# Attention values by quarters of the array: 128 keys from two blocks, two banks

## The chip, the cores and the metric

One core of a Trainium2 chip runs the whole program. The metric is the device time of one execution in microseconds (us), the median over the runs. The profile is that of one further execution; its span runs from the first to the last instruction.

## The reference, cut to what matters

Attention over a sliding window of 128 keys with a linear distance penalty, followed by a feed-forward block with squared ReLU, all in fp32:

```python
B, H, S, D = 8, 8, 576, 64
mask = (rel >= 0) & (rel < 128)              # rel = query position - key position
scores = where(mask, q @ k.T / sqrt(D) + bias, -1e9)
attn = softmax(scores)
x = (attn @ v)            # -> [B*S, 512] = [4608, 512]
h = relu(x @ w_in)        # w_in  [512, 2048]
out = (h * h) @ w_out     # w_out [2048, 512]
```

## The kernel before, in words

The 4608 tokens of all batches are cut into 9 chunks of 512 (`c`), the 8 heads into 4 pairs (`p`), the 2048 hidden columns into 16 tiles (`f`). A chunk and a pair make a **couple** `q = 4c + p`, which holds two **segments** of 256 tokens (`sg` 0 and 1). There are 36 couples. In a segment a tile of 128 tokens (`i` = 0, 1) for each head (`j` = 0, 1) attends to 128 keys for every token: those of its own 128-key block up to its own place, and the later part of the block before.

The feed-forward part is `gemm1(c, f)`, 12 matmuls of 512 columns into the PSUM tile `g` (pool `g1`, one bank), and `gemm2(c, f)`, 12 matmuls in four groups `m` of three, into four PSUM tiles `acc`. After `gemm1`, ScalarE takes the ReLU of `g` (L178), VectorE squares it (L184), ScalarE casts the high part `hh` (L186), VectorE subtracts for the low part `hl` (L188). Both GEMMs run in fp32r with such splits. The other PSUM pools are `sc` (two banks, tile `s` or `S`), `at` (one bank) and `ac` (four).

The first four couples and the next four run in `start`, from a plan with costs and due times. From then on the loop over `t` in `tile_attn_moe` sets TensorE's order by hand: an even `t` is a `gemm1`, an odd `t` the `gemm2` of two tiles earlier. Eight steps of `t` make one **round**, in which one couple passes through. In the round's step `part == 0` come, ahead of `gemm2`: `both`, which computes the values of the couple whose softmax is done (28 couples go this way, from couple 8 on); the loads of the couple after next; and `Couple.front`, the scores and the softmax of the next couple (27 couples). At `part` 3 and 5 `middle` transposes a segment's probabilities on TensorE (L302), ScalarE copies them to `own` (L309), and two GpSimd selects make `prev` (L312) and `own` (L318), zero outside the window. The other engines' instructions are ordered by the framework.

`mix` (L327 to L338) computes the values: for each tile `i` and head `j` one matmul with the 128 keys of the block before (`prev`) and one with the 128 keys of the own block (`own`), each of 128 token columns, 64 output rows, all 128 rows of the array. The two heads use the two column halves. An fp32 product stands in the trace as two matmul records, called passes here. `both` then casts the high part of the result on ScalarE (L359) and subtracts for the low part on VectorE (L360); tile `xu` is what `gemm1` reads.

`Couple.scores` computes products of 64 rows by 64 output rows with 64, 128 or 192 columns, in a **quarter** of the array each: `h` picks the output half, `j` (the head) the row half. The list of each quarter is laid end to end by columns, `at` being the place where a product begins, and all are issued in the order of `at`. The scores of segment 1 that stand in `base` share the bank `G` (from pool `g1`) between both heads: `shared`. So that two row halves never write it together, the second head's first product in it waits for a GpSimd nop (L412) that waits for the first head's last (`done`). Blocks that lie in another batch's window are left out (`late`), so that couples come in seven kinds, three or four couples of each.

ScalarE then copies the base scores to SBUF (L441, L448), VectorE folds in the rest (L460, L464), finds the row maxima (L276), ScalarE exponentiates (L283), VectorE inverts the sums (L290, L291), GpSimd normalises (L294).

Of the kernel before, what the change touches and what calls it, by code (L numbers as in the profile page):

```python
# [9 lines left out]
F32 = mybir.dt.float32  # L10
F32R = mybir.dt.float32r
# [3 lines left out]
ALU = mybir.AluOpType  # L15
# [5 lines left out]
NP = H // 2  # L21
# [12 lines left out]
LATER = [("z", 7)]  # L34
RING = lambda k: 55 + 10.5 * (k - 8)
CONV = lambda f: 36 + 6 * f
FIRST = 35
SYNC = mybir.DependencyInfo(mybir.DependencyClass.Sync, mybir.DependencyReason.DATA)
CST = 256 + 128 * H
ENGINES = {e: getattr(mybir.EngineType, e) for e in ("PE", "DVE", "Activation", "Pool", "SP")}  # L40
# [6 lines left out]
class Kern:  # L47
# [67 lines left out]
    def load_qk(self, c, p, sg):  # L115
# [7 lines left out]
            to, of = to[:, a:e], of[:, a:e]  # L123
        self.nc.sync.dma_start(to, of)

    def load_v(self, c, p):
        self.v[c, p] = self.room(c, p, "v", [128, 5, 128], 4608)
        a = 0 if c else 128
        self.nc.sync.dma_start(self.v[c, p].rearrange("p n d -> p (n d)")[:, a:640], self.vd[c, p][:, a:640])
# [31 lines left out]
    def gemm1(self, c, f):  # L161
        nc = self.nc
        xs = [self.x[c, p] for p in range(NP)]
        g = self.g1.tile([128, 512], F32, name="g")
        wh, wl = self.w[f][:, 0, :, 1], self.w[f][:, 0, :, 0]
        i = 0
        for cc in range(NCC):
            for w, part in ((wh, 0), (wh, 1), (wl, 0)):
                nc.tensor.matmul(  # L169
                    g, w[:, cc * 128 : cc * 128 + 128], xs[cc][:, part], start=i == 0, stop=i == 11  # L170
                )
                i += 1
        yield
        r = self.hp.tile([128, 512], F32, name="r", bufs=1)
        hh = self.hp.tile([128, 512], F32R, name="hh")
        hl = self.hp.tile([128, 512], F32R, name="hl")
        self.h[c, f] = hh, hl
        nc.scalar.activation(r, g, AF.Relu)  # L178
        if c == 0:
            yield  # L180
            nc.scalar.activation(r, r, AF.Square)
        else:
            yield
            nc.vector.tensor_tensor(r, r, r, op=ALU.mult)  # L184
        yield
        nc.scalar.copy(hh, r)  # L186
        yield
        nc.vector.tensor_tensor(hl, r, hh.bitcast(F32), op=ALU.subtract)  # L188

    def gemm2(self, c, f):  # L190
        nc = self.nc
        hh, hl = self.h.pop((c, f))
        if f == 0:
            self.acc = self.start_banks if c == 0 else [self.ac.tile([128, 512], F32, name="acc") for _ in range(4)]
        wh, wl = self.w[f][:, 1, :, 1], self.w[f][:, 1, :, 0]
        for m in range(4):
            ms = slice(m * 128, m * 128 + 128)
            for i, (w, h) in enumerate(((wh, hh), (wh, hl), (wl, hh))):
                nc.tensor.matmul(  # L199
                    self.acc[m], w[:, ms], h, start=(f == 0 and i == 0), stop=(f == NF - 1 and i == 2)  # L200
                )
            if f == NF - 1:
                o = self.op.tile([128, 512], F32, name="o")
                out = self.outd[m * 128 : m * 128 + 128, 512 * c : 512 * c + 512]
                if c == NCH - 1 and m == 3:
                    nc.scalar.copy(o[:, 0:256], self.acc[m][:, 0:256])
                    nc.vector.tensor_copy(o[:, 256:512], self.acc[m][:, 256:512])
                    nc.sync.dma_start(out[:, 0:256], o[:, 0:256])
                    nc.scalar.dma_start(out[:, 256:512], o[:, 256:512])
                    continue  # L210
                (nc.scalar.copy if m % 2 else nc.vector.tensor_copy)(o, self.acc[m])
                nc.sync.dma_start(out, o)


class Segment:
# [86 lines left out]
            self.nc.tensor.transpose(self.z[:, m], self.t[:, m], self.K.ident)  # L302

    def place(self):
        pp = self.K.pp.tile([128, 1024], F32, name="pp")
        self.own, self.prev = (pp[:, a : a + 512].rearrange("p (m c) -> p m c", c=128) for a in (0, 512))

    def out(self):
# [40 lines left out]

    def both(self, other):
        K = self.K
        X = K.at.tile([128, 512], F32, name="at")
        for s in (self, other):
            s.X = X[:, 256 * s.sg : 256 * s.sg + 256]
            s.mix(s.sg == 0)
        u = K.x[self.c, self.p] = K.xu.tile([128, 2, 512], F32R, name="xu")
        self.nc.scalar.copy(u[:, 0], X)  # L359
        self.nc.vector.tensor_tensor(u[:, 1], X, u[:, 0].bitcast(F32), op=ALU.subtract)  # L360

    def soft(self):
        for m in range(4):
# [2 lines left out]
        self.sums()  # L366
        self.norm()

    def middle(self):
        self.turn()  # L370
        self.out()
        self.before()
        self.same()


class Couple:
# [11 lines left out]
    def scores(self):  # L388
        K, nc = self.K, self.nc
        self.S = K.sc.tile([128, 2, 512], F32, name="s")  # L390
        self.G = K.g1.tile([128, 512], F32, name="g")
        todo = []
        for h in range(2):
            base, extra = (h, h + 1), (2 - 2 * h,)
            for j in range(2):
                first = [(0, i, p) for i in range(2) for p in ([(0, 1, 2)] if h == 0 else [base, extra])]
                shared, rest = ([(1, i, p) for i in range(2)] for p in (base, extra))
                at = 0
                for s, i, part in shared + first + rest if j == 0 else first + rest + shared:
                    blocks = [x for x in part if x >= self.both[s].late.get(2 * i + h, 0)]  # L400
                    if blocks:
                        to, n = self.spot(s, j, i, part == extra), len(blocks)
                        a = 64 * (blocks[0] - part[0])
                        todo.append((at, h, j, s, i, blocks[0], n, to[64 * h : 64 * h + 64, a : a + 64 * n], s == 1 and part == base))
                        at += 64 * n
        done = None
        qk = K.qk[self.both[0].c, self.both[0].p]
        for at, h, j, s, i, a, n, to, shared in sorted(todo, key=lambda y: y[:3]):
            u, r = 4 * s + 2 * i + h, slice(64 * j, 64 * j + 64)
            q0, k0 = 64 * u + 640 * s, 256 + 64 * (u + a)  # L410
            if shared and j == 1 and done:
                turn = nc.gpsimd.nop()  # L412
                K.tc.add_manual_dep(turn.ins, done.ins.name, SYNC, reason="one head at a time in the shared bank")
            mm = nc.tensor.matmul(  # L414
                to, qk[r, q0 : q0 + 64], qk[r, k0 : k0 + 64 * n], start=True, stop=True, skip_group_check=True,
            )
            if shared and j == 0:
                done = mm
            elif shared and done:
                K.tc.add_manual_dep(mm.ins, turn.ins.name, SYNC, reason="one head at a time in the shared bank")  # L420
                done = None
# [173 lines left out]
def start(K):  # L595
# [31 lines left out]
    for k in range(18):  # L627
# [19 lines left out]
        else:  # L647
# [6 lines left out]
                P.add(n("e", m), "Activation", 0.4, (n("t", m),) + ((n("e", m - 1),) if m else ()), d + 0.5, do(G.exp, m))  # L654
            P.add(n("r"), "DVE", 0.4, (n("e", 3),), d + 1, G.sums)
            P.add(n("n"), "Pool", 1.05, (n("r"),), d + 1, G.norm)
            if k > 16:
                continue
            P.add(n("z"), "PE", 0.55, (n("n"),) + chain("z"), d + 1, G.turn, ("at", "pp"), "t")
            P.add(n("o"), "Activation", 0.6, (n("z"),), d + 1, G.out, None, "at")  # L660
            P.add(n("p"), "Pool", 0.72, (n("o"),), d + 1.5, G.before)
            P.add(n("m"), "Pool", 0.66, (n("p"),), d + 1.5, G.same)
            if k > 15:
                continue
            P.add(n("x"), "PE", 1.1, (n("m"), ("v", c, p)) + chain("x"), d + 2, G.values, "at", "pp")
            P.add(n("h"), "Activation", 0.4, (n("x"),), d + 2, G.high)
            P.add(n("l"), "DVE", 0.36, (n("h"),), d + 2, G.low, None, "at")
# [27 lines left out]
def tile_attn_moe(ctx: ExitStack, tc: tile.TileContext, *aps):  # L695
    K = Kern(ctx, tc, *aps)
    K.const()
    with tc.manual_schedule(engines={ENGINES["PE"]}):
# [3 lines left out]
        for n in range(NF, NF * NCH + 2):  # L702
            for t in (2 * n, 2 * n + 1):
                q, part = divmod(t - FIRST, 8)
                q += 9
                with tc.high_priority(offset=50):
                    if part == 0:
                        if q - 1 in pairs:
                            first, second = pairs.pop(q - 1)
                            first.both(second)  # L710
                        if q + 1 < 4 * NCH:
                            K.load(*divmod(q + 1, 4))
                        if q < 4 * NCH:
                            C = Couple(K, q)
                            C.front()
                            pairs[q] = C.both
                    if part in (3, 5) and q in pairs:
                        pairs[q][part // 4].middle()
                if t % 2 == 0 and n < NF * NCH:
                    for _ in K.gemm1(*divmod(n, NF)):  # L720
                        pass
                if t % 2:
                    K.gemm2(*divmod(n - 2, NF))


def _consts():
# [16 lines left out]
def _arrays(q, k, v, moe_w_in, moe_w_out):  # L743
# [6 lines left out]
    ], axis=2) for c in range(NCH)])  # L750
    vt = np.zeros((NP, 1 + B * S // 128, 128, 128), np.float32)
    vt[:, 1:] = v.reshape(B, NP, 2, S, D).transpose(1, 0, 3, 2, 4).reshape(NP, B * S // 128, 128, 128)
    vd = np.stack([vt[:, 4 * c : 4 * c + 5].transpose(0, 2, 1, 3).reshape(NP, 128, 640) for c in range(NCH)])
    w1d = a(moe_w_in.reshape(NCC, 128, NF, 128).transpose(2, 1, 0, 3).reshape(NF, 128, NCC * 128))
    return [a(qkd), a(vd), w1d.view(np.int64), a(moe_w_out).view(np.int64), _consts()]

# [17 lines left out]
```

## Time and profile before

| what | us |
|---|---|
| median of 3 runs | 997.23 (997.16 to 998.27) |
| the profiled execution | 996.04 |
| its span | 994.2 |
| TensorE busy | 984.2 (99%) |
| VectorE, ScalarE, GpSimd busy | 438.4, 453.7, 191.8 |

The busy share of TensorE is modelled, since the ends of pipelined matmuls are; the starts of its records show its pace. The profiled execution is 1.84 us longer than its span.

### The profile page before, as it was taken

The numbers are of one execution on the slowest core, as the hardware profiler recorded it, in microseconds if no ns is written. First come the engines' busy times: TensorE is split into PE (matmuls) and PEld (weight loads), VectorE is DVE, ScalarE is ACT, GpSimd is POOL, SyncE is SP. The second block draws the span as 40 slices with busy tenths as digits, with TensorE's granted clock in tenths as the row PEclk, the third lists the DMA queues.
The fourth block names the chain that finished last, engine by engine and source line by source line (L and its number), as shares of the span: only waits on it lengthen the run. The fifth ranks groups of instructions, "written<-read, shape, count | busy, mean of one in ns | idle before, by whom it ended". The sixth has DMA issues, their size and how long they took to land.

```text
span 994.2 us, 16896 instructions
## 1 busy us (share of the span) xinstructions
PE 984.2 (99%) x6545; PEld 814.1 (82%) x6548; DVE 438.4 (44%) x1269; ACT 453.7 (46%) x1180; POOL 191.8 (19%) x252
## 2 busy tenths in 40 slices
PE   9899999999999999999999999999999999999998
PEld 5678788888888888888888888888888888888886
DVE  6889824444443434344444344333434444422222
ACT  7899744444433444344444343334444444422221
POOL 4132321221112222222212211122222221100000
PEclk9999999999999999999999999999999999999999
DMA  9971202111211002111211121110111110001001
GB/s 350 404 276 53 63 14 80 38 39 38 80 38 39 26 20 73 39 38 38 81 38 38 38 80 38 38 39 19 65 35 39 38 57 1 1 1 43 1 1 42
DMA packets 26943, 61.50 MB, mean 62 GB/s; under 512 B 2928, under 2 KB 4336, under 8 KB 26864
## 3 DMA queue, kind: packets, MB, share of 16 engines
q1 hardware_dynamic: 26432, 59.91, 17.4%
q8 instruction: 51, 0.84, 0.3%
q10 hardware_dynamic: 432, 0.52, 0.2%
q14 instruction: 28, 0.23, 0.1%
HBM read 50.99 MB, written 9.44 MB: 61 GB/s over the span
## 4 chain that ended last, share of the span: by engine, by line
PE 97%; DVE 1%; ACT 1%; issue 0%; POOL 0%; DVEq 0%; POOLq 0%; ACTq 0%
PE acc L199 41%; PE g L169 40%; PE at L335 6%; PE at L302 3%; PE s L414 2%; PE g L414 2%; PE g L105 1%; PE s L239 1%; PE acc L335 1%; PE at L530 0%; PE s L498 0%; PE acc L498 0%; PE acc L533 0%; DVE tw L508 0%; ACT w L155 0%
## 5 line engine op out<-in xcount | busy, mean ns | idle before, releaser
L169 PE MATMUL g<-xu,w 128*128 128x512 f32 x1728 | 433.9, 400 | 2.6 <-ACT r L178 2.6
L199 PE MATMUL acc<-hh,w 128*128 128x512 f32 x1152 | 388.7, 398 | 0.0
L169 PEld LDWEIGHTS g<-xu,w 128*128 128x128 f32 x1728 | 333.3, 196 | 65.3 <-ACT r L178 3.3
L199 PEld LDWEIGHTS acc<-hh,w 128*128 128x128 f32 x1152 | 224.8, 195 | 46.1 <-issue 1.5
L184 DVE TENSOR_TENSOR r<-r 128x512 f32<-128x512 f32 x128 | 88.6, 692 | 342.3 <-ACT r L178 340.4
L199 PE MATMUL acc<-hl,w 128*128 128x512 f32 x576 | 227.6, 395 | 0.0
L178 ACT ACTIVATE r<-g 128x512 f32<-128x512 f32 x144 | 85.5, 594 | 299.5 <-PE g L169 299.2
L188 DVE TENSOR_TENSOR hl<-r,hh 128x512 fp32r<-128x512 f32 x144 | 102.2, 710 | 108.9 <-ACT hh L186 104.7
L186 ACT CAST hh<-r 128x512 fp32r<-128x512 f32 x144 | 89.2, 619 | 95.0 <-DVE r L184 94.5
L199 PEld LDWEIGHTS acc<-hl,w 128*128 128x128 f32 x576 | 112.5, 195 | 20.4
L294 POOL TENSOR_TENSOR t<-t,nm 128x512 f32<-128x512 f32 x64 | 81.1, 1267 | 239.2 <-DVE nm L291 214.2
L283 ACT ACTIVATE t<-t,nm 128x128 f32<-128x128 f32 x256 | 99.5, 390 | 35.2 <-DVE nm L276 35.0
L312 POOL TENSOR_SCALAR_AFFINE_SELECT pp<-pp 128x512 f32<-128x512 f32 x64 | 43.4, 679 | 185.7 <-ACT pp L309 185.6
L335 PEld LDWEIGHTS at<-pp,v 128*64 128x64 f32 x1024 | 55.2, 137 | 12.7 <-issue 12.0
L335 PE MATMUL at<-pp,v 128*64 128x128 f32 x1024 | 63.8, 276 | 0.0
L309 ACT COPY pp<-at 128x512 f32<-128x512 f32 x72 | 42.1, 584 | 45.5 <-PE at L302 44.5
L276 DVE CUSTOM_DVE_ANT_0 t<-t,cst 128x128 f32<-128x128 f32 x256 | 59.2, 293 | 1.0
L450 POOL MEMSET t<- 64x128 f32 (+1 forms) x35 | 8.1, 232 | 236.3 <-PE g L414 235.9
L460 DVE COPY_PREDICATED t<-cst,s 64x256 f32<-64x256 int32 x85 | 37.8, 445 | 32.4 <-ACT t L448 19.1
L283 ACT ACTIVATION_READ_ACCUMULATOR t<-t,nm 128x1 f32 x256 | 48.0, 187 | 0.0
L318 POOL TENSOR_SCALAR_AFFINE_SELECT pp<-pp 128x512 f32<-128x512 f32 x64 | 42.3, 661 | 4.4
L414 PE MATMUL s<-qk 64*64 64x64 f32 (+2 forms) x988 | 40.2, 253 | 0.0
(71 smaller groups left out, 587.4 us busy)
## 6 DMA issues: line engine op xcount, KB each, us to landing
raw<-in_dram SPq DMA_DIRECT2D x32, 512.0 KB, 8.9
qk<-in_dram SPq DMA_DIRECT2D x32, 320.0 KB, 3.5
v<-in_dram SPq DMA_DIRECT2D x32, 320.0 KB, 3.0
qk<-in_dram SPq DMA_DIRECT2D x38, 256.0 KB, 3.8
out_dram<-o SPq DMA_DIRECT2D x35, 256.0 KB, 2.7
v<-in_dram SPq DMA_DIRECT2D x3, 256.0 KB, 5.0
wide<-in_dram SPq DMA_DIRECT2D x3, 256.0 KB, 5.2
qk__200<-in_dram SPq DMA_DIRECT2D x2, 256.0 KB, 5.6
```

The costliest lines, as they stand in the source:

```text
L169: nc.tensor.matmul(g, w[:, cc * 128 : cc * 128 + 128], xs[cc][:, part], start=i == 0, stop=i == 11)
L178: nc.scalar.activation(r, g, AF.Relu)
L184: nc.vector.tensor_tensor(r, r, r, op=ALU.mult)
L186: nc.scalar.copy(hh, r)
L188: nc.vector.tensor_tensor(hl, r, hh.bitcast(F32), op=ALU.subtract)
L199: nc.tensor.matmul(self.acc[m], w[:, ms], h, start=(f == 0 and i == 0), stop=(f == NF - 1 and i == 2))
L276: self.nc.vector.tensor_tensor_reduce(self.t[:, m], self.t[:, m], self.K.nrel(2 * self.p + m // 2), -0.125, BIG, ALU.add, ALU.min, self.nm ...
L283: self.nc.scalar.activation(self.t[:, m], self.t[:, m], AF.Exp, bias=nm[:, m : m + 1], scale=-1.0, accum_out=nm[:, 4 + m : 5 + m],)
L294: self.nc.gpsimd.tensor_tensor(self.t, self.t, self.nm[:, 8:12].unsqueeze(2).to_broadcast([128, 4, 128]), op=ALU.mult)
L312: self.nc.gpsimd.affine_select(self.prev, self.own, pattern=[[0, 4], [-1, 128]], compare_op=ALU.is_gt, fill=0.0, base=0, channel_multiplier=1,
L335: self.nc.tensor.matmul(self.X[r, o : o + 128], v[:, 2 * sg + k, r], src[:, j], start=start and n == 0, stop=n == 3 - self.skip, skip_grou ...
L414: mm = nc.tensor.matmul(to, qk[r, q0 : q0 + 64], qk[r, k0 : k0 + 64 * n], start=True, stop=True, skip_group_check=True,)
```

## The change

- The values are computed in two kinds of product. `wholes`: the own block, one product of 128 rows and 128 columns for each `i` and `j`, as before. `corners`: the block before is no longer multiplied in 128 rows. For each `i`, `j` and each half `h` of the rows one product of 64 rows, 64 output rows and 64 columns, so that one token half meets one key half. Corners of `h` = 0 go to the bank `X`, in which the wholes are added; those of `h` = 1 go to a second bank `Y`, taken from the pool `g1`.
- For every token half, the probabilities for 128 keys from two blocks now lie in `own` and in the new tile `rest`, which four smaller GpSimd selects in `halves` make out of `own`, in place of two in `middle`.
- The values `vd` of chunks 2 and up are stored so that rows 64 and up of each block hold those of the block one earlier.
- `both` evacuates by two more steps: VectorE copies `Y` to SBUF (`first`) and adds half of `X` to it, ScalarE copies the other half of `X`; then the cast and the subtraction as before, now out of SBUF. `hl` of the `gemm1` just ahead is ordered behind `first`.
- `both` and `front` move from ahead of `gemm2` to behind its first group of three matmuls, and a round begins two steps of `t` later (`FIRST`). `middle` of segment 16 moves from `start` into the loop.
- In `Couple.scores` the head that uses the shared bank first is now `j` = 1, and its shared products stand behind one other product in the list.

```diff
-FIRST = 35
+FIRST = 37
+ORDER = mybir.DependencyInfo(mybir.DependencyClass.NoSync, mybir.DependencyReason.SCHED_ONLY)
...
+    def parts(self, s):
+        return s.pp[:, 512:768].rearrange("p (m c) -> p m c", c=64)
...
+    def halves(self):
+        nc = self.nc
+        self.turn()
+        self.out()
+        self.rest = self.K.parts(self)
+        for to, of, sign in ((self.rest, self.own, 1), (self.own, self.own, -1)):
+            for h in range(2):
+                r, c = slice(64 * h, 64 * h + 64), slice(64 * h, 64 * h + 64)
+                d = sign * (1 - 2 * h)
+                nc.gpsimd.affine_select(
+                    to[r] if to is self.rest else to[r, :, c], of[r, :, c], pattern=[[0, 4], [-d, 64]],
+                    compare_op=ALU.is_gt if d > 0 else ALU.is_ge, fill=0.0, base=0, channel_multiplier=d,
+                )
+    def corners(self, X, Y):
+        K, sg = self.K, self.sg
+        v, rest = K.v[self.c, self.p], self.rest.rearrange("p (j i) c -> p j i c", j=2)
+        for i in range(2):
+            n = 2 * sg + i
+            for h, to, k in ((0, X[:, 256 * sg + 128 * i :], n), (1, Y[:, 128 * sg + 64 * i :], (n + 2) % 5)):
+                r = slice(64 * h, 64 * h + 64)
+                for j in range(2):
+                    d = slice(64 * j, 64 * j + 64)
+                    self.nc.tensor.matmul(
+                        to[d, 0:64], v[r, k, d], rest[r, j, i], start=h == 1 or n == 0, stop=True, skip_group_check=True,
+                    )
+    def wholes(self, X):
+        K, sg = self.K, self.sg
+        v, own = K.v[self.c, self.p], self.own.rearrange("p (j i) c -> p j i c", j=2)
+        for i in range(2):
+            n = 2 * sg + i
+            for j in range(2):
+                d = slice(64 * j, 64 * j + 64)
+                self.nc.tensor.matmul(
+                    X[d, 128 * n : 128 * n + 128], v[:, n + 1, d], own[:, j, i], start=False, stop=True,
+                    skip_group_check=True,
+                )
     def both(self, other):
...
+        Y = K.g1.tile([128, 512], F32, name="g")
+        u = K.x[self.c, self.p] = K.xu.tile([128, 2, 512], F32R, name="xu")
+        low = K.op.tile([128, 512], F32, name="o")
         for s in (self, other):
-            s.X = X[:, 256 * s.sg : 256 * s.sg + 256]
-            s.mix(s.sg == 0)
-        u = K.x[self.c, self.p] = K.xu.tile([128, 2, 512], F32R, name="xu")
-        self.nc.scalar.copy(u[:, 0], X)
-        self.nc.vector.tensor_tensor(u[:, 1], X, u[:, 0].bitcast(F32), op=ALU.subtract)
+            s.corners(X, Y)
+        for s in (self, other):
+            s.wholes(X)
+        part = lambda x, h: x.rearrange("p (n c) -> p n c", c=128)[:, :, 64 * h : 64 * h + 64]
+        first = nc.vector.tensor_copy(part(low, 1), Y[:, 0:256].rearrange("p (n c) -> p n c", c=64))
+        K.tc.add_manual_dep(K.last_low.ins, first.ins.name, ORDER, reason="the scores wait for it")
+        nc.vector.tensor_tensor(part(low, 1), part(X, 1), part(low, 1), op=ALU.add)
+        nc.scalar.copy(part(low, 0), part(X, 0))
+        nc.scalar.copy(u[:, 0], low)
+        nc.vector.tensor_tensor(u[:, 1], low, u[:, 0].bitcast(F32), op=ALU.subtract)
...
-                for s, i, part in shared + first + rest if j == 0 else first + rest + shared:
+                for s, i, part in rest[:1] + shared + first + rest[1:] if j == 1 else first + rest + shared:
...
-            if shared and j == 1 and done:
+            if shared and j == 0 and done:
...
-                    if part in (3, 5) and q in pairs:
-                        pairs[q][part // 4].middle()
+                parts = K.gemm2_parts(*divmod(n - 2, NF))
+                next(parts)
+                with tc.high_priority(offset=50):
+                    if part == 0 and q - 1 in pairs:
+                        first, second = pairs.pop(q - 1)
+                        first.both(second)
...
+                for _ in parts:
+                    pass
...
+    vd[2:, :, 64:] = np.roll(vd[2:, :, 64:], 1, axis=3)
```

## Rows read from the trace of the kernel before

**Rows 1.** The page: chain of work that ended last, by engine.
```profile
PE 97%; DVE 1%; ACT 1%; issue 0%; POOL 0%; DVEq 0%; POOLq 0%; ACTq 0%
```

**Rows 2.** TensorE's timeline in one round: start, length, line, tile, shape, count.
```profile
502.89 1.97 PE L335 MATMUL at<-pp,v 128*64 128x128 f32 x32
504.78 0.32 PE L414 MATMUL g<-qk 64*64 64x128 f32 x1
...
506.15 0.51 PE L199 MATMUL acc<-hh,w 128*128 128x512 f32 x1
...
514.65 0.60 PE L302 MATMUL at<-cst,t 128*128 128x128 f32 x4
```

**Rows 3.** The chain in the same round, in order of time.
```profile
512.01 2.80 PE acc L199 x12
```

**Rows 4.** TensorE's timeline where the values of a single segment run.
```profile
92.23 1.09 PE L335 MATMUL at<-pp,v 128*64 128x128 f32 x16
93.26 0.76 PE L239 MATMUL s<-qk 64*64 64x192 f32 x16
```

**Rows 5.** ScalarE's timeline in the round of rows 2.
```profile
502.99 0.60 ACT L178 ACTIVATE r<-g 128x512 f32<-128x512 f32 x1 [3.62 <-PE g L169]
```

**Rows 6.** VectorE's timeline in the same round.
```profile
503.62 0.69 DVE L184 TENSOR_TENSOR r<-r 128x512 f32<-128x512 f32 x1 [3.53 <-ACT r L178]
```

**Rows 7.** Groups by line and shape: busy us, mean ns of one.
```profile
L186 ACT CAST hh<-r 128x512 fp32r<-128x512 f32 x144 | 89.2, 619 | 95.0 <-DVE r L184 94.5
...
L537 DVE COPY pp<-acc 128x256 f32<-128x256 f32 x4 | 1.7, 422 | 0.2
```

**Rows 8.** Who waited for whom: us in all, times, longest.
```profile
ACT t L441 <- DVE t L464: 9.6, 15, 1.0
```

**Rows 9.** Scores alone, one couple of six kinds: window, length, busy (records), weight loads.
```profile
156.60:158.14 1.54, 1.52 (x52) 1.41 (x52) 1.00 0.25 43
236.88:238.30 1.42, 1.40 (x52) 1.29 (x52) 1.00 0.32 67
343.90:345.40 1.50, 1.48 (x48) 1.31 (x48) 1.00 0.19 55
451.38:452.80 1.42, 1.40 (x52) 1.30 (x52) 1.00 0.25 32
...
665.74:667.26 1.52, 1.50 (x52) 1.39 (x52) 1.00 0.29 56
773.01:774.66 1.65, 1.64 (x56) 1.52 (x56) 1.00 0.30 68
```

**Rows 10.** TensorE's timeline inside the scores of the last kind.
```profile
773.02 0.32 PE L414 MATMUL g<-qk 64*64 64x128 f32 x1
...
773.40 0.28 PE L414 MATMUL g<-qk 64*64 64x128 f32 x2
...
773.91 0.32 PE L414 MATMUL g<-qk 64*64 64x128 f32 x1
```

**Rows 11.** TensorE's timeline at segment 0's transposes: four kinds.
```profile
193.26 0.60 PE L302 MATMUL at<-cst,t 128*128 128x128 f32 x4
...
246.66 0.65 PE L302 MATMUL at<-cst,t 128*128 128x128 f32 x4
...
461.16 0.60 PE L302 MATMUL at<-cst,t 128*128 128x128 f32 x4
...
783.13 0.60 PE L302 MATMUL at<-cst,t 128*128 128x128 f32 x4
```

**Rows 12.** GpSimd's timeline: the normalising step that those transposes read.
```profile
191.49 1.04 POOL L294 TENSOR_TENSOR t<-t,nm 128x512 f32<-128x512 f32 x1 [6.98 <-DVE nm L291]
...
245.57 1.04 POOL L294 TENSOR_TENSOR t<-t,nm 128x512 f32<-128x512 f32 x1 [7.34 <-DVE nm L291]
...
458.82 1.04 POOL L294 TENSOR_TENSOR t<-t,nm 128x512 f32<-128x512 f32 x1 [6.14 <-DVE nm L291]
...
781.17 1.04 POOL L294 TENSOR_TENSOR t<-t,nm 128x512 f32<-128x512 f32 x1 [7.01 <-DVE nm L291]
```

More of the change, by code (lines that the diff above doesn't have):

```diff
@@ L187, in gemm1, with gemm2_parts @@
         yield
-        nc.vector.tensor_tensor(hl, r, hh.bitcast(F32), op=ALU.subtract)
+        self.last_low = nc.vector.tensor_tensor(hl, r, hh.bitcast(F32), op=ALU.subtract)
     def gemm2(self, c, f):
+        for _ in self.gemm2_parts(c, f):
+            pass
+    def gemm2_parts(self, c, f):
         nc = self.nc
@@ L209, in gemm2 @@
                     nc.scalar.dma_start(out[:, 256:512], o[:, 256:512])
-                    continue
-                (nc.scalar.copy if m % 2 else nc.vector.tensor_copy)(o, self.acc[m])
-                nc.sync.dma_start(out, o)
+                else:
+                    (nc.scalar.copy if m % 2 else nc.vector.tensor_copy)(o, self.acc[m])
+                    nc.sync.dma_start(out, o)
+            yield
 class Segment:
@@ L304, in place @@
     def place(self):
-        pp = self.K.pp.tile([128, 1024], F32, name="pp")
+        self.pp = pp = self.K.pp.tile([128, 1024], F32, name="pp")
         self.own, self.prev = (pp[:, a : a + 512].rearrange("p (m c) -> p m c", c=128) for a in (0, 512))
@@ L352, in both @@
+    def wholes(self, X):
[9 more added lines that the diff above has]
+                )
     def both(self, other):
-        K = self.K
+        K, nc = self.K, self.nc
@@ L367, in soft @@
         self.norm()
[L369 to L373, printed above, removed]
 class Couple:
@@ L416, in scores @@
             )
-            if shared and j == 0:
+            if shared and j == 1:
                 done = mm
@@ L656, in start @@
             P.add(n("n"), "Pool", 1.05, (n("r"),), d + 1, G.norm)
-            if k > 16:
+            if k > 15:
                 continue
@@ L662, in start @@
             P.add(n("m"), "Pool", 0.66, (n("p"),), d + 1.5, G.same)
-            if k > 15:
-                continue
             P.add(n("x"), "PE", 1.1, (n("m"), ("v", c, p)) + chain("x"), d + 2, G.values, "at", "pp")
@@ L706, in tile_attn_moe @@
                 with tc.high_priority(offset=50):
[L707 to L710, printed above, removed]
+                    if part in (3, 5) and q in pairs:
+                        pairs[q][part // 4].halves()
+                if t % 2 == 0 and n < NF * NCH:
+                    for _ in K.gemm1(*divmod(n, NF)):
+                        pass
+                if t % 2 == 0:
+                    continue
+                parts = K.gemm2_parts(*divmod(n - 2, NF))
[4 more added lines that the diff above has]
+                        first.both(second)
                         if q + 1 < 4 * NCH:
@@ L716, in tile_attn_moe @@
                             pairs[q] = C.both
-                    if part in (3, 5) and q in pairs:
-                        pairs[q][part // 4].middle()
[L719 to L723, printed above, removed]
+                for _ in parts:
+                    pass
 def _consts():
@@ L752, in _arrays @@
     vt[:, 1:] = v.reshape(B, NP, 2, S, D).transpose(1, 0, 3, 2, 4).reshape(NP, B * S // 128, 128, 128)
-    vd = np.stack([vt[:, 4 * c : 4 * c + 5].transpose(0, 2, 1, 3).reshape(NP, 128, 640) for c in range(NCH)])
+    vd = np.stack([vt[:, 4 * c : 4 * c + 5].transpose(0, 2, 1, 3) for c in range(NCH)])
+    vd[2:, :, 64:] = np.roll(vd[2:, :, 64:], 1, axis=3)
+    vd = vd.reshape(NCH, NP, 128, 640)
     w1d = a(moe_w_in.reshape(NCC, 128, NF, 128).transpose(2, 1, 0, 3).reshape(NF, 128, NCC * 128))
```

## Prediction

> **What bounds the kernel now.** I read the chain that ended last first: 97% of it is TensorE [rows 1], so a change is worth what it takes from, or adds to, TensorE's own sequence, and a stall of another engine counts only where TensorE runs into it. Next I read TensorE's timeline through one round [rows 2]. The reader should see that it has no holes to fill: values from 502.89, scores from 504.78, `gemm2` from 506.15, then two GEMM steps, then segment 0's transposes at 514.65. A full GEMM step of twelve matmuls takes 2.80 us [rows 3], three of them 0.70. The rest of the views are for the places where the new sequence could meet something that is not ready: the other engines' timelines just behind `gemm1` [rows 5, 6], the scores of the different kinds of couple [rows 9, 10], and the transposes with what they wait for [rows 11, 12].
>
> **The values.** Before, they take 504.78 - 502.89 = 1.89 us for 32 passes of 128 columns [rows 2]; the values of a single segment take 93.26 - 92.23 = 1.03 us for 16 [rows 4]. The difference, 0.86 for 16 passes, is 0.108 for a pair of passes that run side by side in the two column halves. What is left of 1.03 after eight pairs is 0.16 and hardly depends on the work; I call it the price of a change of array shape. The wholes of both segments are exactly such a stage: 16 passes of 128 columns, 1.03 us.
>
> The corners are 16 products, 32 passes of 64 columns, eight in each quarter. No stage of before has only these. Scores run in the same four quarters, and there 704 columns in the fullest quarter, two passes each, fit in about 1.25 us of a stage (below), which is the same 0.11 per pass of 128 columns with all four quarters going at once. Half of it and a little for the start gives 0.057, an estimate: 8 x 0.057 = 0.46. With a change of shape, 0.15, that is 0.61. Bounds: 0.44 (half of 0.108, eight times) and 0.91 (only two quarters at once); I take the low side, because the scores show four.
>
> One wait joins it. `Y` lies in the bank that `gemm1` has just filled, so the first corner with `h` = 1 needs the ReLU to be done with it. In the round of rows 2 the ReLU ends at 503.59 [rows 5], and the first corner, three matmuls later than the old values, would start at 502.89 + 0.70 = 503.59 too. A wait that ends in another engine costs 0.03 to 0.05: VectorE's start at 503.62 behind that ReLU [rows 5, 6], and transposes that start at 246.66 behind GpSimd's end at 245.57 + 1.04 = 246.61 [rows 11, 12]. I take 0.05; it is 0 if corners with `h` = 0 fill the time.
>
> Sum: 1.89 - (0.61 + 0.05 + 1.03) = 0.20 to 0.22 us less for each couple, and 28 couples: 6.0 us less.
>
> The Trainium skill, TensorEngine Tiling (Array Packing), section Tiling Modes, says that a change of tiling mode, not only of the tile, drains the engine. That speaks against this change, which adds one such change per round; the trace agrees, since the 0.16 that is left of each stage is in the sum already.
>
> **The evacuation.** `first` on VectorE is 256 columns out of PSUM, 0.42 [rows 7]. It can start when the corners end and the square of 0.69 that begins at 503.62 [rows 6] is over: about 504.4, and ends near 504.8. The scores, whose bank `G` is that bank again, start at 503.59 + 1.69 = 505.3. So `first` is hidden with some 0.4 to spare, and GpSimd's selects (halves of shapes it had) end several us before the corners read them. `hl` then waits for `first`, and `hl` is needed a GEMM step later. The rest of the chain is longer than before: `hl` 0.7, the add 0.4, ScalarE's copy of half of `X`, the cast of 0.62 [rows 7]. The trace shows ScalarE wait for a VectorE read of the same PSUM tile in the folds of the scores [rows 8], and the add and the copy both read `X`, so I put them one behind the other. The cast then ends around 0.2 us after ScalarE could have begun on the new scores. If the framework puts the cast ahead of them, the softmax begins up to 0.2 later; if behind, 0. I take 0.1.
>
> **The scores.** A stage is the fullest quarter's passes in a row (0.057, 0.109 and 0.163 for 64, 128, 192 columns), 0.05 at the first pass of a quarter that stood still (0.32 against 0.28 for 128 columns [rows 10]), and 0.10 at the end. For the kind of 236.88, 704 columns: 1.21 + 0.15 = 1.36, which the row confirms (1.40, to the modelled end of the last product) [rows 9]. Longer is the kind of 343.90, with as many columns but fewer records: there the wait for the shared bank counts. In the kind of 773.01 the bank's second user starts at 773.91, 0.51 after the start of the first user's last product at 773.40 [rows 10]; laid out by the rule, everything issued up to that product ends 0.12 before. Issue is in order, so all four quarters stand meanwhile. With 0.115 for this hand-over, the rule gives all seven kinds to 0.01.
>
> In the new order the first user's products stand 64 columns later in their lists, and the second user's first product comes at 384 to 512 columns as before. Laid out again, the issue stops at about 0.9 to 0.98 us into the stage in most kinds. Worked out for the kind of 236.88: the product ahead of `done` in the order has 192 columns, its second pass starts at 0.54 and ends at 0.86, the hand-over makes it 0.98; the fullest quarter has 256 columns left, 0.05 + 0.45, plus 0.10: 1.58, where it was 1.36. In order of time the kinds change by +0.11 (three couples), +0.21, -0.07, +0.10, +0.14, +0.11 and +0.03 (four each): 2.4 us more in all. Bounds: 0 if the hand-over were free, 4 if it grew by half.
>
> **The transposes.** Between the scores and segment 0's transposes now lie nine matmuls of `gemm2` and two GEMM steps, 0.70 less than before. So the softmax has 0.70 less time. In the kind of 236.88 the normalising step ends at 246.61 and the transposes start at 246.66: no slack at all [rows 11, 12]. Its four couples will wait 0.70 + 0.1. In the kind of 183 the slack is 193.26 - 192.53 = 0.73, less 0.05 for the wait's end: 0.02 short of nothing, so its three couples wait the 0.1. The kinds of 451 and 773 have 1.30 and 0.92 and keep 0.5 and 0.2. In all 4 x 0.8 + 3 x 0.1 = 3.5 us more; bounds 2.8 and 4.2 by the evacuation's 0 and 0.2.
>
> **Nothing** for `FIRST`, for the four transposes that move from `start` into the loop (the same passes in a sequence that is full on both sides), for the loads (two GEMM steps later, as are their readers) and for `vd`. The last round ends long before the last chunk's GEMMs, and `xu` is needed two GEMM steps after its stage.
>
> **Sum.** 6.0 - 2.4 - 3.5 = 0.1 us faster. The profiled execution would go from 996.04 to 995.9, the median, which is 1.19 higher, from 997.23 to 997.1. A difference below 0.2%, 2 us, can hardly be told from none here.
>
> **The rivals.**
> 1. *The waits are not there.* If the softmax gains back its 0.7 (its ScalarE work now meets other work of the GEMMs) or the hand-over hides, only the values' 6.0 and part of the 5.9 count: 3 to 6 us faster, 991 to 994. For it: idle time on all engines but TensorE. Against it: a slack of 0.05 in four couples.
> 2. *The softmax starts later* (slower). Copy, cast and subtraction stand on ScalarE and VectorE ahead of the base copies and folds. Each further 0.1 us costs ten or eleven couples 0.1, 1 us; from 0.3 us on top of the 0.1 it decides for slower, and at 0.5 it is 5 us: 1002. For it: both engines take instructions in order and the evacuation has two more steps. Against it: base copies can't start before the scores' end, and by then most of it is over.
> 3. *Short products don't start faster* (slower). If passes of 64 columns could not follow each other faster than the mean of a score stage, 1.40/52 = 0.027 [rows 9], the corners' 32 would take 0.86, 0.40 more, times 28: 11 us, 1008. Against it: the kind of 343.90 takes longer with 48 records than that of 236.88 with 52, so the count does not set the time. The Trainium skill, TensorE: Matmul & The Clock Gate, section "Wait — 56ns, not 53.3ns?", states such a floor, a start every 25 ns however few the columns. By it the corners would take 0.80 and the sum would be some 9.5 us slower.
>
> **Chances.** My forecast 0.47; rival 1 0.26; rival 2 0.20; rival 3 0.07. The forecast's own range, from the bounds of its terms, is 995 to 999.5. Over all cases the range is 991.8 to 1001.5, which leaves out rival 3, the far end of rival 2 and the best of rival 1. Faster by over 0.2%: 0.28 (rival 1 and a little of the forecast); within: 0.46; slower: 0.26.
>
> **What would show it.** Right: values and corners together 1.65 to 1.7 us from the first corner to the first score; the first score product in `G` not waiting for VectorE; score stages of 1.5 to 1.6 us with a hole at 0.9; transposes that start 0.05 behind the normalising step in the couples of the second kind. Wrong: 32 corner passes that take 0.8 us or more; the scores' start released by `first`; transposes waiting in most couples, or in none. The prediction fails upward if the softmax's start slips by 0.3 us, downward if those four couples' normalising ends earlier than the scores' end plus 7.7 us.

## The result, and the profile after

The changed kernel takes 998.61 us (median of 20 runs, 997.05 to 1000.08) where the kernel before, on the same chip, takes 996.38 (994.81 to 998.27). The ratio is 1.0021 [1.0014, 1.0028]: 2.1 us slower by the ratio (2.2 between the medians), just beyond the 0.2% that I had called no change, and not the 0.1 us faster that the sum gave. The time is inside the predicted range, but it went up and not down. The profiled execution of the changed kernel has a span of 996.8 us, the kernel before 994.2.

To see where the 2.6 us of span come from I cut TensorE's sequence in the loop into stages, each from its first matmul to the first of the next stage. "Rest" is what the GEMM steps and the transposes take over 2.80 us a step and 0.110 us a transpose, from 100 us on, so it holds TensorE's waits.

| us, summed over the loop | forecast change | before | after | change |
|---|---|---|---|---|
| values (28 couples) | -6.0 | 53.13 | 49.94 | -3.2 |
| scores (27 couples) | +2.4 | 39.29 | 42.16 | +2.9 |
| rest | +3.5 | 6.48 | 9.42 | +2.9 |
| sum | -0.1 | | | +2.6 |

The three terms have the forecast's signs. The scores are 0.5 above it and the rest 0.6 below it; that these two misses nearly cancel is luck. The values give half of what they should, and that decides the sign of the sum.

The page's chain by engine, after, beside [rows 1]:

```profile
PE 93%; ACT 3%; DVE 2%; issue 1%; DMA 1%; POOL 0%; SPq 0%; DVEq 0%; ACTq 0%; POOLq 0%
```

Four points of the chain have gone from TensorE to the others. The chain now runs through softmaxes, because TensorE waits for them in some couples (below).

TensorE's timeline in the round that answers to [rows 2] (start, length, line, tile, shape, count):

```profile
511.91 0.40 PE L207 MATMUL acc<-hh,w 128*128 128x512 f32 x1
512.24 0.33 PE L385 MATMUL at<-pp,v 64*64 64x64 f32 x4
512.39 0.27 PE L385 MATMUL g<-pp,v 64*64 64x64 f32 x2
...
513.00 1.09 PE L396 MATMUL at<-pp,v 128*64 128x128 f32 x16
514.02 0.37 PE L466 MATMUL s<-qk 64*64 64x192 f32 x3
```

Corners from 512.24, wholes from 513.00, scores from 514.02: 0.76 + 1.02 = 1.78 us. The forecast was 0.66 + 1.03, in place of 1.89 before. In the two corner lines (L385) the reader should see the tiles: `X` (`at`) starts at 512.24, `Y` (`g`) only 0.15 later.

ScalarE and VectorE at the same place, beside [rows 5, 6]:

```profile
511.65 0.60 ACT L182 ACTIVATE r<-g 128x512 f32<-128x512 f32 x1 [3.62 <-PE g L173]
```

```profile
512.28 0.69 DVE L188 TENSOR_TENSOR r<-r 128x512 f32<-128x512 f32 x1 [3.53 <-ACT r L182]
513.11 0.42 DVE L412 COPY o<-g 128x256 f32<-128x256 f32 x1
```

The ReLU ends at 511.65 + 0.60 = 512.25. VectorE, which waits for it too, is there at 512.28, 0.03 later; the first product in `Y` at 512.39, 0.14 later. The copy out of `Y` ends at 513.53, 0.5 before the scores: it is hidden, as forecast.

What lies between the ReLU's end and the first product in `Y` stands in the queue of the weight loads: the first weight load for `Y`, and the list of the semaphore instructions on the corners' line (count, shortest/median/longest in ns, first and last start):

```profile
512.36 0.17 PEld L385 LDWEIGHTS g<-pp,v 64*64 64x64 f32 x2
```

```profile
L385 PEldq EVENT_SEMAPHORE  x56: 51/51/51, 156.7 to 888.1; - x56
```

There are two separate semaphore instructions of 51 ns in each of the 28 couples. One of them is over 4.2 us before the first corner. The other waits for ScalarE: in this couple it starts at 512.28, 0.04 behind the ReLU's end, and ends at 512.33; the weight load follows 0.03 later, the product another 0.03 later.

The scores alone, one couple of each kind of [rows 9] (window, length, busy with records, weight loads, clock, DMA share, GB/s):

```profile
162.73:164.42 1.69, 1.68 (x52) 1.30 (x52) 1.00 0.27 43
243.39:245.05 1.66, 1.65 (x52) 1.36 (x52) 1.00 0.34 42
353.86:355.32 1.46, 1.44 (x48) 1.31 (x48) 1.00 0.24 35
460.55:462.09 1.54, 1.52 (x52) 1.38 (x52) 1.00 0.27 45
674.58:676.27 1.69, 1.67 (x52) 1.49 (x52) 1.00 0.33 65
782.26:783.99 1.73, 1.71 (x56) 1.53 (x56) 1.00 0.37 46
```

As forecast, all kinds but the third are longer and the third is shorter. From the first product to the next stage the seven kinds take 1.61, 1.60, 1.38, 1.46, 1.61, 1.62 and 1.65; the sum had 1.60, 1.58, 1.39, 1.47, 1.59, 1.59 and 1.63. The hole at 0.98 is there too, in the second kind's stage, which starts at 243.41:

```profile
243.92 0.27 PE L466 MATMUL g<-qk 64*64 64x128 f32 x1
243.94 0.47 PE L466 MATMUL s<-qk 64*64 64x192 f32 x9
244.41 0.32 PE L466 MATMUL g<-qk 64*64 64x128 f32 x1
```

The shared bank's second user starts at 244.41, 1.00 us into the stage.

Segment 0's transposes in the same couple, TensorE and GpSimd, beside [rows 11, 12]:

```profile
252.58 0.40 PE L207 MATMUL acc<-hh,w 128*128 128x512 f32 x1
253.40 0.66 PE L311 MATMUL at<-cst,t 128*128 128x128 f32 x4 [0.43 <-POOL t L303]
```

```profile
252.31 1.04 POOL L303 TENSOR_TENSOR t<-t,nm 128x512 f32<-128x512 f32 x1 [7.40 <-DVE nm L300]
```

The normalising step ends at 253.35 and the transposes start 0.05 later, behind a wait. The GEMM step ahead of them takes 3.39, 3.39, 3.74 and 3.39 us in the four couples of this kind, not 2.80: 2.7 us, nearly all of the rest's 2.9. The first kind hardly waits (0.05 at most). From the scores' end to these transposes pass 8.40 us in both kernels (238.26 to 246.66 before, 245.00 to 253.40 after), although TensorE has 0.70 less to do in between: the softmax sets the time.

### The profile page after: what moved, and what is told of

It is laid out like the page before. It is cut to its first block, busy times and chain, and to the rows that moved or that the text cites. A ratio compares the mean times of both kernels' runs of the same rounds, so it can differ in the third digit from the quotient of the medians.

```text
span 996.8 us, 18025 instructions
## 1 busy us (share of the span) xinstructions
PE 984.8 (99%) x6993; PEld 810.2 (81%) x6996; DVE 463.5 (46%) x1325; ACT 466.5 (47%) x1208; POOL 215.7 (22%) x364
## 4 chain that ended last, share of the span: by engine, by line
PE 93%; ACT 3%; DVE 2%; issue 1%; DMA 1%; POOL 0%; SPq 0%; DVEq 0%; ACTq 0%; POOLq 0%
PE g L173 39%; PE acc L207 39%; PE at L311 3%; PE at L396 2%; PE s L466 2%; PE g L466 1%; PE g L385 1%; PE at L344 1%; PE at L385 1%; ACT t L292 1%; ACT t L500 1%; PE s L248 1%; PE acc L344 1%; DMA qk<-in_dram 1%; DVE t L512 1%
## 5 line engine op out<-in xcount | busy, mean ns | idle before, releaser
L207 PE MATMUL acc<-hh,w 128*128 128x512 f32 x1152 | 393.4, 399 | 0.0
L188 DVE TENSOR_TENSOR r<-r 128x512 f32<-128x512 f32 x128 | 91.4, 714 | 297.0 <-ACT r L182 295.4
L192 DVE TENSOR_TENSOR hl<-r,hh 128x512 fp32r<-128x512 f32 x144 | 107.5, 747 | 87.6 <-ACT hh L190 84.0
L303 POOL TENSOR_TENSOR t<-t,nm 128x512 f32<-128x512 f32 x64 | 77.3, 1208 | 244.6 <-DVE nm L300 236.7
L371 POOL TENSOR_SCALAR_AFFINE_SELECT pp<-pp 64x256 f32<-64x256 f32 x224 | 101.3, 452 | 130.3 <-ACT pp L318 119.3
L466 PE MATMUL s<-qk 64*64 64x64 f32 (+2 forms) x988 | 43.4, 257 | 0.0
L466 PEld LDWEIGHTS s<-qk 64*64 64x64 f32 x988 | 37.6, 133 | 4.6 <-issue 4.6
L311 PEld LDWEIGHTS at<-cst,t 128*128 128x128 f32 x256 | 31.4, 140 | 12.0 <-POOL t L303 4.7
L311 PE MATMUL at<-cst,t 128*128 128x128 f32 x256 | 38.7, 274 | 2.0 <-POOL t L303 2.0
```

What stands on the lines that cost most here:

```text
L192: self.last_low = nc.vector.tensor_tensor(hl, r, hh.bitcast(F32), op=ALU.subtract)
L207: nc.tensor.matmul(self.acc[m], w[:, ms], h, start=(f == 0 and i == 0), stop=(f == NF - 1 and i == 2))
L303: self.nc.gpsimd.tensor_tensor(self.t, self.t, self.nm[:, 8:12].unsqueeze(2).to_broadcast([128, 4, 128]), op=ALU.mult)
L371: nc.gpsimd.affine_select(to[r] if to is self.rest else to[r, :, c], of[r, :, c], pattern=[[0, 4], [-d, 64]], compare_op=ALU.is_gt if d > ...
L466: mm = nc.tensor.matmul(to, qk[r, q0 : q0 + 64], qk[r, k0 : k0 + 64 * n], start=True, stop=True, skip_group_check=True,)
```

## The experiments

All ratios are to the kernel before on the same chip. My theory: three separate losses, the hand-over of bank `Y`, the new list of the scores, and the transposes that come too early, each of which can be undone alone. The rivals: that the corners themselves are dear (short products don't run faster), and that the softmax is late for the evacuation, not for the 0.70.

**The old list of the scores.**

```
-                for s, i, part in rest[:1] + shared + first + rest[1:] if j == 1 else first + rest + shared:
+                for s, i, part in shared + first + rest if j == 0 else first + rest + shared:
-            if shared and j == 0 and done:
+            if shared and j == 1 and done:
-            if shared and j == 1:
+            if shared and j == 0:
```

> The changed kernel with the old order of the scores' lists: head 0 uses the shared bank first and its shared products stand first in its list, head 1's last. Theory A (the bank's hand-over between the heads made the scores longer): the score stages go back to 1.36 to 1.60 us, 2.9 us less over 27 couples, nothing else moves, and the time falls from 2.1 us above the kernel before to about 0.8 below it. Rival B (VectorE's copy of the second bank holds the scores back, and the new order was hiding that): the first product in the shared bank now waits for that copy, the stages stay at 1.5 us or more, and the time stays within 1 us of the changed kernel.

Measured: 997.14 against 995.95, 1.0011 [1.0003, 1.0020]: slower than the kernel before, where I had expected 0.8 us faster. The scores fall to 39.27, all of the 2.9, as theory A has it and against rival B. But the rest rises to 10.37, where theory A had nothing else move. ScalarE in the couple of the second kind, and TensorE where that couple's scores end:

```profile
244.12 0.62 ACT L416 CAST xu<-o 128x512 fp32r<-128x512 f32 x1
244.65 1.02 ACT L500 COPY t<-g 64x128 f32<-64x128 f32 x3
```

```profile
244.39 0.51 PE L207 MATMUL acc<-hh,w 128*128 128x512 f32 x1
```

The cast still runs when the scores end at 244.39, and the copies that start the softmax begin 0.26 later. In the changed kernel the same copies begin 0.12 after the scores' end at 245.00, and the cast (244.50 + 0.62) ends just as they begin:

```profile
244.50 0.62 ACT L416 CAST xu<-o 128x512 fp32r<-128x512 f32 x1
245.12 1.02 ACT L500 COPY t<-g 64x128 f32<-64x128 f32 x3
```

So the longer scores hid the evacuation, and rival 2 is real once they are short: the four couples of the second kind wait another 0.10 to 0.13 each, half of the rest's 0.95. The other half is spread over many steps by hundredths, and I didn't follow it.

**The transposes two parts later.**

```
-                    if part in (3, 5) and q in pairs:
-                        pairs[q][part // 4].halves()
+                    if part in (5, 7) and q in pairs:
+                        pairs[q][part // 6].halves()
```

> The changed kernel with both segments' transposes one GEMM pair later in the round (parts 5 and 7 for 3 and 5). Theory A (the softmax had 0.7 us less time and the transposes waited for it): the waits of 0.59 us in three couples and 0.94 in one are gone, 2.5 to 2.7 us less, so the time is about 0.5 us below the kernel before. Rival D (those waits are given back elsewhere, because the corners then wait for GpSimd's selects of segment 1): the corners start later and the time does not fall.

Measured: 996.56, 1.0008 [0.9999, 1.0017], not the 0.5 us below the kernel before that I had expected. The waits of the second kind are gone: the normalising step of the couple shown above now ends 5 us before its transposes.

```profile
250.36 1.04 POOL L303 TENSOR_TENSOR t<-t,nm 128x512 f32<-128x512 f32 x1 [7.39 <-DVE nm L300]
```

```profile
256.55 0.60 PE L311 MATMUL at<-cst,t 128*128 128x128 f32 x4
```

The rest falls from 9.42 to 7.28, by 2.1 of the 2.7. Of the 0.6 that is missing, 0.31 is one GEMM step at 301.90, in the couple whose wait was 0.94: there the GEMM's ReLU runs behind six exponentials and ends at 304.97, and the next `gemm1` starts at 305.02. I didn't follow what is left. Values and scores are as after (49.95, 42.16), so the corners don't wait for the later selects (rival D). The loss of the second kind belongs to where the transposes stand.

**Two groups of `gemm2` ahead of the corners.** The ReLU then ends 0.7 before the first corner.

```
                 next(parts)
+                next(parts)
```

> The changed kernel with values and scores behind the second group of three matmuls of the GEMM step, not the first. Theory A (the corners of the second bank wait for the ReLU that empties it, 0.15 us each time): that wait goes, the corners fall from 0.76 to 0.61 us, 4.2 us in all; but the softmax has another 0.69 us less, and the transposes wait 0.6 to 1.3 us in some eleven couples, some 7 us more, so the time is about 5 us above the kernel before. Rival C (passes of 64 columns, or the added change of array shape, are that slow by themselves): the corners stay at 0.76, and the time is some 9 us above.

Measured: 1011.21, 1.0157 [1.0141, 1.0173]. The corners go to 0.625 us (0.61 expected) and the values to 46.19 in all. This is against rival C, by which the corners stay at 0.76. The loss against the kernel before, 15.3 us, is three times what I expected, for the rest rises to 27.13. ScalarE, VectorE, GpSimd and TensorE in one couple show why:

```profile
170.45 0.39 ACT L292 ACTIVATE t<-t,nm 128x128 f32<-128x128 f32 x1
...
170.95 0.60 ACT L182 ACTIVATE r<-g 128x512 f32<-128x512 f32 x1
171.44 0.39 ACT L292 ACTIVATE t<-t,nm 128x128 f32<-128x128 f32 x1
```

```profile
171.58 0.69 DVE L188 TENSOR_TENSOR r<-r 128x512 f32<-128x512 f32 x1 [0.92 <-ACT r L182]
172.19 0.16 DVE L299 TENSOR_SCALAR nm<-nm 128x4 f32<-128x4 f32 x1
```

```profile
172.74 1.04 POOL L303 TENSOR_TENSOR t<-t,nm 128x512 f32<-128x512 f32 x1 [7.85 <-ACT t L292]
```

```profile
173.84 0.66 PE L311 MATMUL at<-cst,t 128*128 128x128 f32 x4 [1.32 <-POOL t L303]
```

The softmax has another 0.70 less, and now the next `gemm1`'s ReLU lands between the exponentials (170.95), and its square takes VectorE ahead of the softmax's sums (171.58, then 172.19). So a softmax that is a little late for the GEMM's next output falls behind it, and another 0.70 lost makes the transposes of three kinds wait 1.2 to 1.5 us longer than in the changed kernel. Of the rest's 17.7 more, 1.6 is no wait: from 318.0 the granted clock is 0.50 (1.2 GHz) for 3.4 us, right behind the longest of these waits, and the `gemm1` step that begins at 317.19 takes 4.45 us, not 2.89. The changed kernel has such a stretch too, from 42.5, ahead of the stages that the table counts.

**Two groups, and the transposes later.** The edits of the last two together.

> Values and scores behind the second group, and the transposes one GEMM pair later. Theory A: no wait for the ReLU (corners 0.61 us, 4.2 us less) and no wait of the transposes (2.7 less), so 4.8 us below the kernel before. Rival C (corners slow by themselves): only the 2.7, half a microsecond below the kernel before.

Measured: 991.07, 0.9954 [0.9942, 0.9967], 4.6 us faster by the ratio, close to the 4.8 expected. Values 46.18, scores 42.18, rest 6.14. TensorE's timeline at the corners:

```profile
508.85 0.27 PE L385 MATMUL at<-pp,v 64*64 64x64 f32 x2
508.87 0.27 PE L385 MATMUL g<-pp,v 64*64 64x64 f32 x2
508.96 0.23 PE L385 MATMUL at<-pp,v 64*64 64x64 f32 x2
508.97 0.23 PE L385 MATMUL g<-pp,v 64*64 64x64 f32 x2
509.02 0.23 PE L385 MATMUL at<-pp,v 64*64 64x64 f32 x2
...
509.31 0.23 PE L385 MATMUL at<-pp,v 64*64 64x64 f32 x2
...
509.48 0.44 PE L396 MATMUL at<-pp,v 128*64 128x128 f32 x4
```

`Y` starts 0.02 behind `X`, not 0.15, and the wholes follow 0.63 after the first corner, not 0.76. This is the same work without the wait: the hand-over of the bank costs 0.135 a couple. The semaphore instructions are all still there:

```profile
L385 PEldq EVENT_SEMAPHORE  x56: 51/430/866, 157.7 to 882.8; - x56
```

But the one that waits for ScalarE now runs 0.66 before the first corner, beside the second group of `gemm2`, and costs nothing.

**The old list, and the transposes later.** The first two edits together.

> Old order of the scores' lists and later transposes, but values and scores behind the first group as in the change, so that the corners still wait for the ReLU. Theory A: 2.9 us for the scores and 2.6 for the transposes against the changed kernel, so 3.4 us below the kernel before, 0.9966, and the corners stay at 0.76 us.

Measured: 993.16 against 995.94, 0.9977 [0.9967, 0.9987], 2.3 us faster by the ratio where I had expected 3.4. The corners stay at 0.76, as expected, and the scores at 39.27. The rest is 7.92, 0.6 above the same kernel with the longer scores, which is part of what the ratio lacks.

**All three edits.**

> Old order of the scores' lists, values and scores behind the second group, transposes one GEMM pair later. Theory A (the three costs are separate: hand-over of the shared bank, wait for the ReLU, wait of the transposes): the score stages fall by 2.9 us in all against the run with the last two alone, so 7.5 us below the kernel before, a ratio of 0.9925. Rival E (the shorter scores are eaten by the evacuation, since ScalarE's cast then stands ahead of the copies of the base scores): the transposes or the next GEMM step wait instead, and the ratio stays near 0.995.

Measured: 989.13 against 995.94, 0.9931 [0.9919, 0.9943], 6.9 us faster by the ratio, of 7.5 expected. Values 46.18, scores 39.29, rest 6.77: the values' gain of 6.95 is there whole, and the other two terms are back at nothing and 0.3.

**The issue order of the scores.** On top of all three, the products of the shared bank's second user are issued last, those of its first user first, so that no quarter stands behind them:

```
-        for ... in sorted(todo, key=lambda y: y[:3]):
+        for ... in sorted(todo, key=lambda y: (y[0] + 1000 * (y[8] and y[2]), not y[8], y[1], y[2])):
```

> The run before this, and the score products are issued in another order: the first head's products of the shared bank ahead of others at the same place, the second head's behind all others; each quarter's own order is unchanged. Theory A (issue is in order, so that the hand-over stops all four quarters): the stages lose most of what is left of the stop, 0.1 us in fifteen couples, 1.2 us in all, 0.9915. Rival F (the stop costs only its own quarter): no difference.

Measured: 992.14, 0.9967 [0.9955, 0.9979]: a miss, 3 us slower than all three alone. The scores rise to 44.44. TensorE in the second kind:

```profile
241.94 0.33 PE L466 MATMUL g<-qk 64*64 64x64 f32 x2
...
242.33 0.87 PE L466 MATMUL s<-qk 64*64 64x192 f32 x25
242.98 0.32 PE L466 MATMUL g<-qk 64*64 64x128 f32 x2
```

The second user's first product starts at 242.98, 1.04 us into the stage, right behind the last start of the 25 records that were issued before it. GpSimd had passed the bank on at 0.70, and by the lists the quarter of the product with 128 columns had worked off what stood before it by then too (an estimate: 384 columns at 0.109 and 0.057 a pass, 0.67 us). I had taken it that a product issued late starts when its quarter and its bank are free; here it starts when all that were issued before it have started.

**Ties in the issue order.** On top of all three, the first user's products go first only where two products have equal places in their lists:

```
-        for ... in sorted(todo, key=lambda y: y[:3]):
+        for ... in sorted(todo, key=lambda y: (y[0], not (y[8] and y[2] == 0), y[1], y[2])):
```

> The run with all three edits, and where several score products stand at the same place of their lists, those of the first head in the shared bank are issued first; no other product moves. Theory A (the hand-over waits for everything issued up to the first head's last product, so that a product of 192 columns in between delays it): the stages of the kinds with such a product ahead fall by 0.07 to 0.09 us, 0.9 us over twelve couples, the others stay. If a product that is issued behind others waits for those to start, as the last run suggests, what was gained is given back by the products that now stand behind, and the stages stay or grow.

Measured: 988.57 against 996.52, 0.9919 [0.9905, 0.9933]. The scores fall to 38.40, 0.07 or 0.10 in each of 12 couples, as expected. The rest rises by 0.6 at the same time, so the gain over all three is small, and the two intervals overlap. Both versions beat the kernel before and the changed one.

## Why the prediction was wrong, step by step

**The step that failed** is the wait for bank `Y`: "I take 0.05". It is 0.135 a couple, 0.760 for the corners with it and 0.625 without it, in otherwise the same stage. From the ReLU's end to the first product in `Y` pass 0.143 to 0.144 us in all 28 couples. Both rows I took the 0.05 from were of other things: a VectorE start behind ScalarE, and transposes behind GpSimd. The same VectorE hand-over is 0.03 here again, and the transposes' 0.05. The sentence that the wait is 0 if the other corners fill the time failed with it: corners in `X` start at 512.24, and the stage is still 0.135 longer. Where the 0.144 goes can be read in the trace: 0.04 to the start of the semaphore instruction, 0.05 for itself, 0.03 to the weight load, 0.03 to the product. The four transposes that wait for GpSimd have no separate semaphore instruction in the 4 us ahead of them, and start 0.05 behind. That this instruction makes the difference is argued, not shown: no run took it away alone, and with two groups it is there at no cost, because it runs 0.66 us before the corners. That the wait costs 0.135 is shown. The corner's base was 0.61 by the sum and 0.625 measured. The two together are 0.10 a couple and, times 28, 2.8 us: all that the values lack (6.0 against 3.2). The 6.0 was itself rounded up: 1.89 - 1.69 = 0.20 a couple gives 5.6, and with that the sum is 0.3 us slower, so the forecast's sign hung on the rounding.

**What was right in the values.** Four quarters run side by side: 64-column passes follow each other in each quarter every 0.058 (six steps from 508.96 to 509.31 with two groups), where I had 0.057. The wholes take 1.02 (1.03).

**Rival 3 falls:** in each of these steps four records start, one every 0.015 us, and all 32 with the change of shape take 0.625. The Trainium skill's floor of 25 ns between starts (TensorE: Matmul & The Clock Gate, section "Wait — 56ns, not 53.3ns?") is not seen where the products go to different quarters.

**The scores** were right in mechanism, in sign for each kind and within 0.03 in a stage's length; the hundredths over 27 couples make most of the 0.5. The old list alone takes exactly this term away.

**The transposes** were right in mechanism and place: the second kind alone, behind the normalising step by 0.05. Each couple waited 0.59 (one of them 0.94, behind a fold that VectorE started 0.35 late, which I didn't follow), where I had 0.8. One 0.1 is the GEMM steps': in the couple shown, in the kernel before, those between scores and transposes take 0.11 less in all (2.76 and not 2.80 for a whole one), so the 0.70 was reckoned from a shorter stretch; why steps run at two paces the record doesn't show. The other, the 0.1 of the evacuation, wasn't paid: the copies that start the softmax begin 0.12 after the scores, as they did before (238.26 and 238.38), since the scores' own lengthening gave the cast time to end. The two terms were summed as if they were independent, and they are not: without the longer scores the 0.1 appears. The first kind's three waits of 0.1 didn't come either.

**The rivals.** Rival 1 (no waits) is excluded by both waits. Rival 2 (a softmax that starts later behind the evacuation) doesn't act in the changed kernel, but it does with the old list, at 0.1 in the couples of the second kind. With two groups the softmax is late for another reason, the GEMM's ReLU and square.

**The bound.** I had counted "within 0.2%" on a sum that was made of three terms of 2 to 6 us, all unsure. The best guess of the wait's size alone moves it by 2.4.

## What to carry to other kernels

When a stage moves next to the work that still holds its buffer, price the hand-over at the engine that waits and in the queue where it waits; a start behind another pair of engines is not a stand-in. Issuing other work first, here three more matmuls, takes the hand-over away, but what then lies closer to its own deadline must be moved as well: alone, the edit that freed 3.8 us in the values added 17.7 us to the rest (9.42 to 27.13, 1.6 of it at the lower clock). Count the slack of each consumer after all moves together, not one term at a time.

## What the runs showed of the hardware

Issue order binds across the four quarters: a product whose quarter (by the lists) and bank are free waits until everything ahead of it has started (1.04 us into the stage instead of 0.70). The Trainium skill says of matmuls packed in the array that they start and end strictly in order (TensorE: Matmul & The Clock Gate, Part 3, section The mechanism); the run agrees for the starts (1.04 us), and the ends of matmuls are only modelled in the trace. The bank that ScalarE hands to TensorE took 0.144 us from the ReLU's end to the first product and cost the corners 0.135, against a start 0.05 behind GpSimd for the transposes.
